# Retention and a bilinear feed-forward layer: another order of loads, transposing DMAs and row stores on SyncE for groups 3 to 10

## The chip, the cores and the metric

The kernel runs on one core of a Trainium2 chip. The metric is the device time of one execution in microseconds (us). Before the change it was 328.05 us, the median of three runs (327.72 to 330.47). TensorE (PE) multiplies matrices into PSUM, VectorE (DVE), ScalarE (ACT) and GpSimd (POOL) do the elementwise work, and SyncE (SP) issues most of the DMAs, in program order.

## The reference

```python
# q, k, v: (8, 8, 576, 64) float32, batch x heads x positions x head_dim
scores = scale * q @ k.transpose(0, 1, 3, 2)
gamma = 1.0 - 2.0 ** (-5.0 - arange(8))
Dmat = where(rel >= 0, gamma[:, None, None] ** rel, 0.0)   # rel = pos[:, None] - pos[None, :]
x = (scores * Dmat) @ v                # to (4608 tokens, 512)
out = ((x @ w_a) * (x @ w_b)) @ w_out  # w_a, w_b: 512 x 1536, w_out: 1536 x 512; out float32
```

## The kernel before

The 4608 tokens are handled in 18 groups of 256 tokens. A group is half of a batch (128 positions twice), except that groups 15 and 17 gather the last 64 positions of four batches each. Groups 0 to 2 are done at the start in another way (the names with `step`), and the others one at a time. The feed-forward layer runs over blocks of tokens: 512, 256, 256, and then seven times 512. In each block twelve rounds of four products `pa` (L745) and four products `pb` (L760) of 128x128 by 512 (or 256) columns give the hidden rows `hT`, and then twelve products `po` (L779) for each 128 tokens give a row block of the output.

Retention is done in chunks of 64 positions. For each group from 3 on these steps are needed:

- `load_pair(n, which)` issues on SyncE the loads of q, k and v into float32 tiles `qf`, `kf`, `vf` (L148): two DMAs of 256 KB for each of the three, one for each 128 rows (`kp`), four for the groups 15 and 17. Each name has four buffers.
- `ahead(n)` casts them on GpSimd to bf16: the lower 64 partitions of q and k as they are (L480), the upper 64 with neighbouring heads exchanged (`upper`, L477), and v scaled by the decay into `vb` (L485). `qkb` and `vb` have three buffers. For k of group 4 the upper half is kept back and cast later by ScalarE, in `upper_keys`.
- `turn(n)` issues two transposing DMAs on SyncE, `qkT` from `qkb`, for q and for k (L498). From group 9 on it also issues the loads of group n + 2 (and for group 9 those of k and v of group 10). `qkT` has three buffers.
- `stretch(into, outof)` is the work of TensorE: for the group `outof`, products with the running states (`open_outputs`, L624); for the group `into`, the key-value sums `kv` (`keyed`, L534) and the scores `sc` (`matched`, L596), the only step that first needs `qkT` of that group; then the products of `outof` with its masked scores (`close_outputs`, L637). What VectorE and ScalarE have to do for it (adding sums, masking, casting states, scaling into `xT`) is put into the list `later`, and is taken from it one entry at a time between the feed-forward products (`pop`).
- `store` writes 128 rows of the output. Rows of blocks 0 to 2 are held back in eight `osb` buffers, and `store_held(rows)` writes them later. In groups 0 to 2 a row block goes out as two DMAs of 128 KB (L701), later as one of 256 KB (L703).

Where these steps stand between the feed-forward products is written out by hand in the list `todo`: a position, counted in products of 512 columns (144 for a block of 512 tokens), and a function. The main loop (from L947) emits the products and runs each entry at the next permitted place (after a `pb` round, or after every fourth `po`) at or beyond its position. The tables `casts` and `turns` give the positions of `ahead` and `turn`. All entries for SyncE, with the stores, form one queue in the order in which they are emitted, and a DMA that must wait for its operand holds back all behind it.

Of the kernel before, what the change touches and what calls it, by code (L numbers as in the profile page):

```python
# [18 lines left out]
def kernel(  # L19
# [10 lines left out]
    nc = tc.nc  # L30

    B, H, S, D = q.shape
    DM = H * D
# [11 lines left out]
    NP = NTOK // 256  # L45
# [12 lines left out]
    def part_of(n):  # L58
        return PAIRS[n][1]
# [106 lines left out]
    Q, K, V = 0, 1, 2  # L166
# [292 lines left out]

        return 8 if n in LEFT else 4 * part_of(n) + i  # L460

    kept = []

    def upper_keys():
        kept.pop()()

    def ahead(n):


        qf, kf, vf = (paired[n].pop(i) for i in (Q, K, V))  # L470
        qkb = nat.tile([128, 2, 2 * DM], BF16, tag="qkb", name="qkb2")
        vb = nat.tile([128, 2 * DM], BF16, tag="vb", name="vb2")
        def upper(w, t, copy):
            to = qkb[64:128, w].rearrange("p (j r d) -> p j r d", r=2, d=D)
            fro = t[64:128].rearrange("p (j r d) -> p j r d", r=2, d=D)
            for r in (0, 1):
                copy(to[:, :, 1 - r], fro[:, :, r])  # L477

        for w, t in ((0, qf), (1, kf)):
            nc.gpsimd.tensor_copy(qkb[0:64, w], t[0:64])  # L480
            if (n, w) == (4, 1):
                kept.append(lambda: upper(1, kf, nc.scalar.copy))
            else:
                upper(w, t, nc.gpsimd.tensor_copy)
        nc.gpsimd.tensor_tensor(  # L485
            vb.rearrange("p (k h d) -> p k h d", k=2, h=H),
            vf.rearrange("p (k h d) -> p k h d", k=2, h=H),
            vs2[:, 2 if n in LEFT else part_of(n)].unsqueeze(3)
            .to_broadcast([128, 2, H, D]),
            op=ALU.mult)  # L490
        natural[FIRST + n, "pair"] = (qkb, vb)
# [417 lines left out]
    def turn_step(i):  # L909
# [3 lines left out]
    todo = [(100, early_casts, ()), (112, turn_step, (4,)),  # L913
            (112.1, cast_step, (5, Q, "act")), (116, score_step, (4,)), (116, state_step, (4,)),
            (124, turn_step, (5,)), (128, output_step, (4,)),
            (128, score_step, (5,)), (128, state_step, (5,)),
            (140, output_step, (5,))]
# [1 line left out]
    todo += [(136, total_of, (2,))]  # L919
    todo += [(28 + 6 * step, pair_tables, (step,)) for step in range(13)]  # L920
    todo += [(170, stretch, (3, None)), (197, stretch, (4, 3)),
             (248, stretch, (5, 4)), (274, open_alone, (5,)),
             (278, close_outputs, (5,)), (336, stretch, (6, None)),
             (372, stretch, (7, 6)), (408, stretch, (8, 7))]
    for n in range(8, NP, 2):
# [3 lines left out]
                 (starts[n] - 44, open_alone, (n + 1,))]  # L929
    todo += [(starts[NP - 2] - 40, close_outputs, (NP - 1,))]  # L930
    placed = {args[0]: at for at, fn, args in todo if fn is stretch}
    casts = {3: 116, 4: 116.15, 5: 175.3, 6: 200, 7: 250, 8: 330}
    turns = {3: 116, 4: 175.1, 5: 175.4, 6: 200.2, 7: 272, 8: 345}
    loads = {9: 345.1}
    todo += [(116.1, load_pair, (4, (K, V))), (175, upper_keys, ()),
             (175.2, load_pair, (5,)), (175.5, load_pair, (6,)), (200.1, load_pair, (7, (Q, K))),
             (200.3, load_pair, (7, (V,))), (200.4, store_held, (4,)),
             (271, load_pair, (8, (Q,))), (272.1, load_pair, (8, (K, V))),
             (272.2, store_held, (2,)), (345.2, store_held, (2,)),
             (345.3, load_pair, (10, (Q,)))]  # L940
    for n in range(9, NP):
        casts[n], turns[n] = placed[n] - 70, placed[n] - 38
    for fn, places in ((ahead, casts), (turn, turns), (load_pair, loads)):
        todo += [(at, fn, (n,)) for n, at in places.items()]
    todo.sort(key=lambda e: e[0])

# [2 lines left out]
    for tb, n in enumerate(blocks):  # L949
        runs = WCOLS if tb == 0 else [1] * NF  # L950
        for cost, edge in ffn_block(tb, tok, n, runs):
            at += cost
            while todo and edge and at >= todo[0][0]:
                _, fn, args = todo.pop(0)
# [33 lines left out]
```

## Time and profile before

| What | Value |
|---|---|
| Median of three runs (lowest, highest) | 328.05 us (327.72, 330.47) |
| The profiled execution's own time, and its span | 326.78 us, 325.0 us |
| TensorE, share of the span | 98% |
| VectorE, ScalarE, GpSimd, share of the span | 50%, 40%, 36% |
| DMA packets of SyncE's queue | 45.37 MB, 69.4% of 16 engines' span |
| Mean DMA rate | 157 GB/s |
| Granted TensorE clock | 1.0 |

The span runs from the first to the last instruction. One product of 512 columns takes 0.216 us when they follow each other (four in 0.86), so 72 positions of `todo` are some 15.6 us, and more with the retention products between them. The trace gives the start of the first score product of each group and the landing of its second transposing DMA:

| Group | `todo` position of its stretch | qkT of k landed, us | first score product, us |
|---|---|---|---|
| 3 | 170 | 54.99 | 57.02 |
| 4 | 197 | 63.07 | 64.45 |
| 5 | 248 | 74.86 | 76.17 |
| 6 | 336 | 90.70 | 97.87 |
| 7 | 372 | 103.70 | 107.54 |
| 8 | 408 | 114.44 | 116.03 |
| 9 | 460 | 129.66 | 129.71 |
| 10 | 532 | 146.06 | 146.10 |
| 11 | 604 | 160.14 | 163.77 |

A line of a timeline reads: start, time that the merged instructions take together, engine and line, operation, output and inputs, shape, count; in brackets the idle time before it and what ended it. A line of the waits reads: who waited for what, us in total, how often, the longest.

### The profile page before, as it was taken

What the parts mean: (1) busy time and instruction counts of PE and PEld (TensorE: products, weight loads), DVE (VectorE), ACT (ScalarE), POOL (GpSimd) and SP (SyncE); (2) the same over time, 40 slices, a digit from 0 to 9 for tenths busy, and PEclk for the clock granted to TensorE, in tenths of its full rate; (3) what the DMA queues carried; (4) which work ended last, traced back from release to release, by engine and by line L of the source; (5) the groups of instructions that cost most, each with busy time, mean ns of one, the idle gap of its engine ahead of it and who ended that gap; (6) DMA issues with size and microseconds to landing.
All of it is one profiled execution on the core that took longest, in us unless ns stands there. A gap on an engine that the chain in (4) does not pass through costs nothing.

```text
span 325.0 us, 8647 instructions
## 1 busy us (share of the span) xinstructions
PE 318.7 (98%) x3611; PEld 164.5 (51%) x3611; DVE 161.6 (50%) x288; ACT 129.5 (40%) x286; POOL 115.5 (36%) x148
## 2 busy tenths in 40 slices
PE   7899999999999999999999999999999999999996
PEld 3564457778444554444454545454445444444444
DVE  6734454665437754735374626561556245414321
ACT  7745753663435533533253324442333233212321
POOL 4990077374642554575274205440520000000000
PEclk9999999999999999999999999999999999999999
DMA  8999999999999999999899169935840620031013
GB/s 217 255 197 207 261 229 200 199 164 216 172 225 200 218 235 243 208 226 229 177 214 194 48 163 199 212 69 145 204 73 22 112 66 0 2 97 32 0 23 109
DMA packets 145431, 50.90 MB, mean 157 GB/s; under 512 B 126704, under 2 KB 140912, under 8 KB 145392
## 3 DMA queue, kind: packets, MB, share of 16 engines
q1 hardware_dynamic: 140112, 45.37, 69.4%
q0 software_dynamic: 4752, 4.72, 8.9%
q8 instruction: 28, 0.46, 0.6%
q10 hardware_dynamic: 528, 0.26, 0.3%
q14 instruction: 11, 0.09, 0.1%
HBM read 37.75 MB, written 9.44 MB: 145 GB/s over the span
## 4 chain that ended last, share of the span: by engine, by line
PE 78%; SPq 9%; DMA 7%; POOL 2%; DVE 1%; issue 1%; ACT 1%; DVEq 0%; ACTq 0%; POOLq 0%
PE po L779 26%; PE pb L760 23%; PE pa L745 22%; SPq L148 5%; DMA qf<-in_q_dram 3%; DMA kf<-in_k_dram 3%; SPq L159 2%; SPq L498 2%; DMA qkT<-qkb 1%; PE o L637 1%; PE o L624 1%; POOL qkb L480 1%; PE sc L596 1%; PE pa L722 1%; POOL qkb L477 1%
## 5 line engine op out<-in xcount | busy, mean ns | idle before, releaser
L765 DVE TENSOR_TENSOR hT<-ha,pb 128x512 bf16<-128x512 bf16 (+1 forms) x120 | 75.9, 634 | 98.0 <-PE pb L760 89.9
L753 ACT CAST ha<-pa 128x512 bf16<-128x512 f32 (+1 forms) x120 | 64.7, 543 | 120.1 <-PE pa L745 117.2
L760 PE MATMUL pb<-xT,wb_sb 128*128 128x512 bf16 (+1 forms) x480 | 111.5, 358 | 0.2
L745 PE MATMUL pa<-xT,wa_sb 128*128 128x512 bf16 (+1 forms) x468 | 108.8, 357 | 0.0
L779 PE MATMUL po<-wo_sb,hT 128*128 128x512 bf16 (+2 forms) x456 | 97.5, 368 | 0.0
L760 PEld LDWEIGHTS <-wb_sb 128*128 128x128 bf16 x480 | 46.9, 98 | 46.8 <-issue 0.5
L745 PEld LDWEIGHTS <-wa_sb 128*128 128x128 bf16 x468 | 45.0, 98 | 44.4 <-issue 0.2
L779 PEld LDWEIGHTS <-hT 128*128 128x128 bf16 x456 | 42.5, 98 | 46.5
L480 POOL CAST qkb<-qf 64x1024 bf16<-64x1024 f32 x15 | 15.5, 1031 | 68.3 <-DMA qf<-in_q_dram 68.3
L485 POOL TENSOR_TENSOR vb<-vf,vs 128x1024 bf16<-128x1024 f32 x15 | 28.5, 1903 | 14.9 <-PE pa L745 7.0
L790 DVE COPY osb<-po 128x512 f32<-128x512 f32 (+2 forms) x17 | 11.1, 652 | 40.4 <-PE po L779 40.4
L788 ACT COPY osb<-po 128x512 f32<-128x512 f32 (+1 forms) x21 | 12.0, 570 | 44.8 <-PE po L779 44.8
L647 DVE TENSOR_TENSOR xT<-o,qs 128x512 bf16<-128x512 f32 x30 | 19.5, 682 | 4.9 <-PE o L637 4.9
L480 POOL CAST qkb<-kf 64x1024 bf16<-64x1024 f32 x15 | 15.8, 1055 | 16.1 <-DMA kf<-in_k_dram 15.6
L559 DVE TENSOR_TENSOR sums<-kv,sums 128x256 f32<-128x256 f32 x44 | 18.6, 424 | 2.8 <-PE kv L534 0.8
L605 DVE TENSOR_TENSOR sT<-sc,mask 128x512 bf16<-128x512 f32 x30 | 19.4, 680 | 0.0
L477 POOL CAST qkb<-qf 64x512 bf16<-64x512 f32 x30 | 17.6, 616 | 0.7
L477 POOL CAST qkb<-kf 64x512 bf16<-64x512 f32 x28 | 16.5, 616 | 0.8
L563 ACT CAST states<-sums 64x512 bf16<-64x512 f32 x26 | 16.0, 617 | 0.3
L311 POOL CAST qkb<-kf 128x512 bf16<-128x512 f32 x5 | 3.1, 617 | 16.8 <-DMA kf<-in_k_dram 16.8
L664 ACT COPY fence<-o 128x2 f32<-128x2 f32 x15 | 2.4, 161 | 15.5 <-PE o L624 15.5
L806 PE MATMUL w<-ones 128*128 128x512 bf16 x19 | 6.9, 483 | 1.5 <-DVE idxp_f L204 1.5
(84 smaller groups left out, 158.4 us busy)
## 6 DMA issues: line engine op xcount, KB each, us to landing
qf<-in_q_dram SPq DMA_DIRECT2D x32, 256.0 KB, 4.7
vf<-in_v_dram SPq DMA_DIRECT2D x32, 256.0 KB, 5.2
kf<-in_k_dram SPq DMA_DIRECT2D x31, 256.0 KB, 5.0
out_dram<-osb SPq DMA_DIRECT2D x25, 256.0 KB, 3.3
out_dram<-osb SPq DMA_DIRECT2D x21, 128.0 KB, 2.4
wo_sb<-in_moe_w_out_dram POOLq DMA_DIRECT2D x3, 512.0 KB, 16.9
qf<-in_q_dram SPq DMA_DIRECT2D x8, 128.0 KB, 3.2
kf<-in_k_dram SPq DMA_DIRECT2D x8, 128.0 KB, 3.4
```

The lines of the kernel that those rows point to most:

```text
L148: nc.sync.dma_start(t[r0:r0 + m, kp * DM:(kp + 1) * DM] .rearrange("p (h d) -> p h d", h=H), src[b, :, s0:s0 + m, :].rearrange("h s d -> s ...
L477: copy(to[:, :, 1 - r], fro[:, :, r])
L480: nc.gpsimd.tensor_copy(qkb[0:64, w], t[0:64])
L485: nc.gpsimd.tensor_tensor(vb.rearrange("p (k h d) -> p k h d", k=2, h=H), vf.rearrange("p (k h d) -> p k h d", k=2, h=H), vs2[:, 2 if n in ...
L559: nc.vector.tensor_tensor(sums[:, i], own, prev, op=ALU.add)
L605: nc.vector.tensor_tensor(sT[:, on].rearrange("p c k s -> p (c k) s"), sc[:, on].rearrange("p c k s -> p (c k) s"), mask3.unsqueeze(1).to_ ...
L647: nc.vector.tensor_tensor(x_of(t0, 128).rearrange("p c (a s) -> p c a s", a=2), o[:, :, :, kp].rearrange("p a c s -> p c a s"), qs[:, :, s ...
L745: nc.tensor.matmul(pa[:, 0:n], wa_sb[:, c, fs], xT[:, c], start=(c == 0), stop=(c == NC - 1))
L753: nc.scalar.copy(ha[:, 0:n], pa[:, 0:n])
L760: nc.tensor.matmul(pb[:, 0:n], wb_sb[:, c, fs], xT[:, c], start=(c == 0), stop=(c == NC - 1))
L765: nc.vector.tensor_tensor(hT[:, F, 0:n], has[F][:, 0:n], pb[:, 0:n], op=ALU.mult)
L779: nc.tensor.matmul(po[:, 0:width], hT[:, F, u * 128:(u + 1) * 128], wo_sb[:, F, cols], start=(F == 0), stop=(F == NF - 1))
```

## The change

Only positions and one cast are changed; every load, transposing DMA, store and product is still made once.

- The order on SyncE. Before: T4 (the two transposing DMAs of group 4), loads of 5, T5, loads of 6, q and k of 7, T6, v of 7, the four held row blocks of block 0, q of 8, T7, k and v of 8, the two row blocks of block 1, T8, loads of 9, the two of block 2, q of 10, three row blocks of block 3, T9, k and v of 10, loads of 11, the last row block of block 3, T10. After: T4, loads of 5, q of 6, T5, k and v of 6, q and k of 7, T6, a row block, v of 7, a row block, q of 8, a row block, k of 8, a row block, v of 8, T7, the two row blocks of block 1, T8, loads of 9, q of 10, the two of block 2, T9, k and v of 10, loads of 11, four row blocks of block 3, T10.
- `casts` and `turns` have the positions that go with it; those of groups 10 and later are the same.
- The cast of k of groups 4 and 5 is made in two halves, each for the 512 columns of one load, with the lower and the two upper casts of a half before those of the next. All are on GpSimd; `upper_keys` on ScalarE is gone.
- The stretch of groups 5 and 4 is placed at 252 instead of 248, that is, after one more round of `pa` and `pb` in a block of 256 tokens.

```diff
@@ -459,29 +459,21 @@
 
         return 8 if n in LEFT else 4 * part_of(n) + i
 
-    kept = []
-
-    def upper_keys():
-        kept.pop()()
-
     def ahead(n):
 
 
         qf, kf, vf = (paired[n].pop(i) for i in (Q, K, V))
         qkb = nat.tile([128, 2, 2 * DM], BF16, tag="qkb", name="qkb2")
         vb = nat.tile([128, 2 * DM], BF16, tag="vb", name="vb2")
-        def upper(w, t, copy):
-            to = qkb[64:128, w].rearrange("p (j r d) -> p j r d", r=2, d=D)
-            fro = t[64:128].rearrange("p (j r d) -> p j r d", r=2, d=D)
-            for r in (0, 1):
-                copy(to[:, :, 1 - r], fro[:, :, r])
-
         for w, t in ((0, qf), (1, kf)):
-            nc.gpsimd.tensor_copy(qkb[0:64, w], t[0:64])
-            if (n, w) == (4, 1):
-                kept.append(lambda: upper(1, kf, nc.scalar.copy))
-            else:
-                upper(w, t, nc.gpsimd.tensor_copy)
+            runs = 2 if (n, w) in ((4, 1), (5, 1)) else 1
+            for i in range(runs):
+                e = slice(i * 2 * DM // runs, (i + 1) * 2 * DM // runs)
+                nc.gpsimd.tensor_copy(qkb[0:64, w, e], t[0:64, e])
+                to, fro = (x.rearrange("p (j r d) -> p j r d", r=2, d=D)
+                           for x in (qkb[64:128, w, e], t[64:128, e]))
+                for r in (0, 1):
+                    nc.gpsimd.tensor_copy(to[:, :, 1 - r], fro[:, :, r])
         nc.gpsimd.tensor_tensor(
             vb.rearrange("p (k h d) -> p k h d", k=2, h=H),
             vf.rearrange("p (k h d) -> p k h d", k=2, h=H),
@@ -919,7 +911,7 @@
     todo += [(136, total_of, (2,))]
     todo += [(28 + 6 * step, pair_tables, (step,)) for step in range(13)]
     todo += [(170, stretch, (3, None)), (197, stretch, (4, 3)),
-             (248, stretch, (5, 4)), (274, open_alone, (5,)),
+             (252, stretch, (5, 4)), (274, open_alone, (5,)),
              (278, close_outputs, (5,)), (336, stretch, (6, None)),
              (372, stretch, (7, 6)), (408, stretch, (8, 7))]
     for n in range(8, NP, 2):
@@ -929,18 +921,20 @@
                  (starts[n] - 44, open_alone, (n + 1,))]
     todo += [(starts[NP - 2] - 40, close_outputs, (NP - 1,))]
     placed = {args[0]: at for at, fn, args in todo if fn is stretch}
-    casts = {3: 116, 4: 116.15, 5: 175.3, 6: 200, 7: 250, 8: 330}
-    turns = {3: 116, 4: 175.1, 5: 175.4, 6: 200.2, 7: 272, 8: 345}
-    loads = {9: 345.1}
-    todo += [(116.1, load_pair, (4, (K, V))), (175, upper_keys, ()),
-             (175.2, load_pair, (5,)), (175.5, load_pair, (6,)), (200.1, load_pair, (7, (Q, K))),
-             (200.3, load_pair, (7, (V,))), (200.4, store_held, (4,)),
-             (271, load_pair, (8, (Q,))), (272.1, load_pair, (8, (K, V))),
-             (272.2, store_held, (2,)), (345.2, store_held, (2,)),
-             (345.3, load_pair, (10, (Q,)))]
-    for n in range(9, NP):
+    casts = {3: 116, 4: 116.15, 5: 141, 6: 200, 7: 253, 8: 283, 9: 376}
+    turns = {3: 116, 4: 116.2, 5: 141.2, 6: 200.2, 7: 253.1, 8: 283.1, 9: 380}
+    todo += [(116.1, load_pair, (4, (K, V))), (116.3, load_pair, (5,)),
+             (141.1, load_pair, (6, (Q,))), (141.3, load_pair, (6, (K, V))),
+             (200.1, load_pair, (7, (Q, K))), (200.3, store_held, (1,)),
+             (200.4, load_pair, (7, (V,))), (200.5, store_held, (1,)),
+             (200.6, load_pair, (8, (Q,))), (200.7, store_held, (1,)),
+             (200.8, load_pair, (8, (K,))), (200.9, store_held, (1,)),
+             (201, load_pair, (8, (V,))), (253.2, store_held, (2,)),
+             (283.2, load_pair, (9,)), (345, load_pair, (10, (Q,))),
+             (345.1, store_held, (2,))]
+    for n in range(10, NP):
         casts[n], turns[n] = placed[n] - 70, placed[n] - 38
-    for fn, places in ((ahead, casts), (turn, turns), (load_pair, loads)):
+    for fn, places in ((ahead, casts), (turn, turns)):
         todo += [(at, fn, (n,)) for n, at in places.items()]
     todo.sort(key=lambda e: e[0])
```

## The prediction

> **What bounds the kernel.** I read the busy shares first, then what TensorE waited for, then the stretches around those waits, and only then SyncE's queue, which the change reorders.
>
> ```profile
> PE 318.7 (98%) x3611; PEld 164.5 (51%) x3611; DVE 161.6 (50%) x288; ACT 129.5 (40%) x286; POOL 115.5 (36%) x148
> ```
>
> TensorE is busy for 98% of the span, so what can be won is what it still waits for:
>
> ```profile
> PE w L806 <- DVE idxp_f L204: 1.5, 1, 1.5
> PE sc L343 <- ACT qkT L330: 0.5, 2, 0.2
> PE sc L596 <- DMA qkT<-qkb: 0.4, 2, 0.3
> ```
>
> The first two lie in the opening 16 us, which the change does not touch. The third does: two times a group's score products (L596) wait for a transposing DMA. Those two are groups 9 and 10. The timeline of TensorE shows group 9, and then group 11, which waits for nothing:
>
> ```profile
> 127.90 1.03 PE L760 MATMUL pb<-xT,wb_sb 128*128 128x512 bf16 x4
> ...
> 129.71 0.45 PE L596 MATMUL sc<-qkT 64*64 64x64 bf16 x32 [0.16 <-DMA qkT<-qkb]
> ...
> 130.35 0.82 PE L745 MATMUL pa<-xT,wa_sb 128*128 128x512 bf16 x3
> ```
>
> ```profile
> 162.30 1.03 PE L760 MATMUL pb<-xT,wb_sb 128*128 128x512 bf16 x4
> ...
> 163.77 0.50 PE L596 MATMUL sc<-qkT 64*64 64x64 bf16 x32
> ...
> 164.49 0.82 PE L745 MATMUL pa<-xT,wa_sb 128*128 128x512 bf16 x3
> ```
>
> From the last four projection products to the first ones after the stretch it is 2.45 us for group 9 (127.90 to 130.35) and 2.19 us for group 11. Group 10 takes 2.58 (144.17 to 146.75), group 8 2.29; undisturbed stretches take 2.19 to 2.30 (groups 7, 11, 12, 13, 14). The waits are therefore worth 0.25 + 0.38 + 0.1 = 0.7 us against 2.20, and 0.4 against 2.30, which is the figure of the wait row. The chain that ended last runs from 94 to 146 us through SyncE's issues, loads and casts, but TensorE is busy beside it: a faster queue wins no more than those 0.4 to 0.7 us.
>
> **The change, part by part.** I follow the second transposing DMA of each group, "Tn", against the score products that need it. Before, they landed / were needed at: T4 63.07 / 64.45, T5 74.86 / 76.17, T6 90.70 / 97.87, T7 103.70 / 107.54, T8 114.44 / 116.03, T9 129.66 / about 129.5, T10 146.06 / about 145.8. These are thin margins, so each reordering is worked out by what it puts ahead of Tn. Three prices, from landings in a busy stretch: a load of 256 KB 1.15 us (group 6: 76.47, 77.67, 78.88, 80.05), a half store of 128 KB 0.31 landing to landing (93.69, 94.00, 94.31) but 0.63 to issue, a transposing DMA 0.8 to 0.9.
>
> *T4 and the casts of k by halves.* SyncE's order is unchanged to the end of group 5's loads. What changes is who casts:
>
> ```profile
> 57.91 1.04 POOL L480 CAST qkb<-kf 64x1024 bf16<-64x1024 f32 x1 [2.38 <-DMA kf<-in_k_dram]
> 61.51 1.91 POOL L485 TENSOR_TENSOR vb<-vf,vs 128x1024 bf16<-128x1024 f32 x1 [2.56 <-PE pa L745]
> ...
> 69.35 1.03 POOL L480 CAST qkb<-kf 64x1024 bf16<-64x1024 f32 x1 [1.21 <-DMA kf<-in_k_dram]
> 70.44 1.18 POOL L477 CAST qkb<-kf 64x512 bf16<-64x512 f32 x2
> ```
>
> A 64x512 cast takes 0.616 and a 64x1024 one 1.035, so a column costs 0.82 ns and an instruction 0.2 us; 64x256, which the trace lacks, comes to 0.4 (GpSimd's 128x256 cast in L393 takes 0.40). A half is 0.62 + 2 x 0.40 = 1.4 us. Group 4's halves of k landed at 56.62 and 57.79: the first half runs 56.7 to 58.1, the second to 59.5. Before, ScalarE's two copies ended at 59.57. T4 is where it was; if the small casts cost 0.62 like the larger, it is 0.9 later and still within 1.4 of cover. GpSimd has 1.8 us more to do, inside its 2.56 us gap before the values. ScalarE loses two copies of 0.61 just before an evacuation that came late: at 60.90 to 61.59 four products took 0.69 where 0.44 is usual. That is worth 0 to 0.25; I take 0.1.
>
> One rule of the Trainium skill speaks against casts on GpSimd: Advanced Engine Details and Errata, Mode Summary, says that the second VectorE port is shared with GpSimd, and that two-port VectorE work and GpSimd block each other. The 64x512 casts here took 616 ns on average for q and for k, beside a VectorE half busy. By the rule T4 could slip by some of its cover; by the rows it does not.
>
> *T5 and the later stretch.* SyncE stands still for T5 before:
>
> ```profile
> 64.31 3.35 SPq L148 DMA_DIRECT2D vf<-in_v_dram  x2
> 68.16 4.74 SPq L498 DMA_TRANSPOSE qkT<-qkb  x2
> 72.94 1.25 SPq L148 DMA_DIRECT2D qf<-in_q_dram  x2
> ```
>
> Of those 4.74 us two issues of 1.3 to 1.8 are work, the rest waits for GpSimd's cast that ends at 71.63. Two loads of group 6 now fill that hole. With the halves the cast runs 68.15 to 69.6 and, k's second half having landed at 69.23, to 71.0. T5 then issues at about 70 and 71.8 and lands at 75.1 to 75.5; if nothing of the hole were used, at 74.86 + 2 x 1.15 = 77.2. The stretch that needs it moves by one pair of 256-column groups, 0.88 us (pb at 74.23 and 75.11): needed at 77.05. What was behind the stretch has one slot less: the four adds, two scalings and two masked copies were done at 83.55 before, which becomes about 84.2; the products that need them start at 85.03. ScalarE's state casts end near 83.0 instead of 83.14, and are read at 83.69. No new stall, but margins of 0.7 and 0.8.
>
> SyncE is at the same place as before at 73.1, two loads ahead: 2.3 us won.
>
> *T6.* The same set of DMAs lies ahead of it: at most 90.70, about 88; needed at 97.87.
>
> *T7.* Four loads of group 8 now lie ahead of it: at most 103.70 + 4 x 1.15 = 108.3, which would be 0.8 late. Against that stand the 2.3 us from T5 and the way the eight half stores are spread:
>
> ```profile
> 89.91 5.99 SPq L701 DMA_DIRECT2D out_dram<-osb  x8
> 95.96 1.30 SPq L148 DMA_DIRECT2D qf<-in_q_dram  x2
> ```
>
> Eight stores took 5.99 us to issue and some 2.6 to move: the DMA share falls to 0.91 in 88 to 96 us, from 1.16 to 1.27 around it. Put between loads, the four store pairs cost little but their 2.6 us. T7 lands at 108.3 - 2.3 - 2.4 = 103.6; 4 us of cover.
>
> The page DMA: Bandwidth & Descriptors, under "Issuing engines are not separate DMA queues", says that the time to issue is usually small beside the transfer. By that rule the interleaving wins nothing and T7 comes at 106.0, still in time; the eight stores above are the opposite case.
>
> *T8, T9, T10.* T8 follows T7 after four half stores (2.5) and two transposings, with its operands long loaded: about 109.5, or 114 with T7 at its bound; needed at 116.03. T9 has the same DMAs ahead of it as before less three stores of block 3 (at least 1.1 by their issue of 0.38), and the wins above: 122 to 128.5; needed at 129.5. T10 keeps its distance to T9 (16.4 us) plus three stores (2): 140, and 145.8 or so from the later bound. So the waits of groups 8 and 9 go for certain, that of group 10 almost so. From T11 on SyncE stands behind block 4's stores, as before (the last issued at 154.47 after ScalarE), and nothing changes.
>
> **Sum.** -0.25 -0.38 (less 0.1 for the 2.30 reading) -0.1 (group 8) -0.1 (ScalarE) = -0.7 us, with bounds of -1.1 and 0 from the rows alone. On the profiled execution: 326.78 - 0.7 = 326.1. Its own time is 1.3 below the median of the three runs, so for the median 328.05 - 0.7, rounded to 327.3. This measurement tells about 1%, 3.3 us, from no change; the forecast is inside that.
>
> **Rivals.**
> 1. *Transposing DMAs late behind loads (slower).* T5 at its bound of 77.2 is 0.1 late. Now and then a load lands 2.3 us after its neighbour instead of 1.15 (66.91 to 69.23, 99.44 to 102.03); one such in front of T5 makes it 1.3 late, and T7 at its bound adds 0.8. That is +2.1 - 0.7 = +1.4: 329.4. It is slower than before from 0.7 us of lateness, and over 1% from 4 us, for which several groups would have to fail. For it: thin margins, three runs spread by 2.7 us. Against: SyncE's idle hole at T5 is seen in the rows, and the moved stretch.
> 2. *No difference.* Groups 9 and 10 still come late by other means (T10's bound), or what TensorE stops waiting for is lost to the slot that the stretch gave up: 328.0.
> 3. *A larger gain.* If the runs that lie 1 to 3.7 us above the profiled execution are slower because T3 to T10 come late in them, wider margins take most of that away: 328.05 - 2 = 326.0.
>
> **Chances.** Forecast 0.58 (326.8 to 327.8), no difference 0.15, larger gain 0.09 (a third of it beyond 1%), slower 0.18 (a third of it beyond 1%). Range: down to the larger gain, 325.8, up past the slower rival, 329.6. Faster by over 1% 0.03, slower by over 1% 0.06, the rest within.
>
> **What would show it.** Right: no wait of L596 for a transposing DMA; the stretches of groups 8 to 10 at 2.2 to 2.3 us; T9 before 129; the transposing pair near 70 us no longer 4.74 us. Wrong: a wait of L596 for T5 at 77 or T7 near 107; L624 waiting for states near 84; or the median moving by more than TensorE's waits do, which would mean that the executions differ in something that the profile of before does not show.

## The result, and the profile after

| | before | after |
|---|---|---|
| Median of 22 executions each, us (lowest, highest) | 329.22 (327.72, 332.0) | 327.48 (326.04, 332.47) |
| Ratio, with its 95% interval | | 0.9952 (0.9929 to 0.9975) |
| The profiled execution, us (span) | 326.78 (325.0) | 327.25 (325.5) |

The kernel is about 0.5% faster, within the 1% that the prediction could not tell from no change, and the time is 0.2 us from the one forecast. Two things do not fit so well. The gain is 1.6 us by the ratio and not 0.7, and the two profiled executions stand the other way round: that of after is 0.5 us longer. The executions of one kernel differ by several microseconds, and the profiled one of before was faster than all 22 in the table.

The busy shares of after, and what TensorE waited for:

```profile
PE 319.0 (98%) x3611; PEld 165.2 (51%) x3611; DVE 162.5 (50%) x288; ACT 128.3 (39%) x284; POOL 117.2 (36%) x156
```

```profile
PE w L798 <- DVE idxp_f L204: 1.5, 1, 1.5
PE sc L588 <- DMA qkT<-qkb: 1.1, 1, 1.1
PE sc L343 <- ACT qkT L330: 0.5, 2, 0.3
```

(The lines have moved by eight: L596 is now L588, L498 is L490.) The score products wait once instead of twice, but longer, 1.1 us against 0.4. TensorE's timeline around the stretches of groups 9 and 10 says which one it is:

```profile
127.80 1.03 PE L752 MATMUL pb<-xT,wb_sb 128*128 128x512 bf16 x4
...
129.27 0.50 PE L588 MATMUL sc<-qkT 64*64 64x64 bf16 x32
129.99 1.04 PE L737 MATMUL pa<-xT,wa_sb 128*128 128x512 bf16 x4
```

```profile
143.82 1.03 PE L771 MATMUL po<-wo_sb,hT 128*128 128x512 bf16 x4
...
146.60 0.45 PE L588 MATMUL sc<-qkT 64*64 64x64 bf16 x32 [1.11 <-DMA qkT<-qkb]
...
147.24 1.04 PE L771 MATMUL po<-wo_sb,hT 128*128 128x512 bf16 x4
```

Group 9 has an undisturbed stretch of 2.19 us (127.80 to 129.99); group 10 takes 3.42 (143.82 to 147.24), 1.2 too long. SyncE's timeline shows why, from group 5 on:

```profile
65.26 3.25 SPq L148 DMA_DIRECT2D vf<-in_v_dram  x2
68.55 1.78 SPq L148 DMA_DIRECT2D qf<-in_q_dram  x2
70.50 4.64 SPq L490 DMA_TRANSPOSE qkT<-qkb  x2
75.19 1.26 SPq L148 DMA_DIRECT2D kf<-in_k_dram  x2
...
122.69 3.66 SPq L490 DMA_TRANSPOSE qkT<-qkb  x2
126.41 1.20 SPq L148 DMA_DIRECT2D kf<-in_k_dram  x2
127.65 2.12 SPq L148 DMA_DIRECT2D vf<-in_v_dram  x2
129.82 2.29 SPq L148 DMA_DIRECT2D qf<-in_q_dram  x2
132.16 3.52 SPq L148 DMA_DIRECT2D kf<-in_k_dram  x2
135.72 2.31 SPq L148 DMA_DIRECT2D vf<-in_v_dram  x2
138.12 2.67 SPq L695 DMA_DIRECT2D out_dram<-osb  x4
140.90 3.36 SPq L490 DMA_TRANSPOSE qkT<-qkb  x2
```

Two readings matter. The pair of transposing DMAs of group 5 takes 4.64 us to issue, as against 4.74 before: SyncE stands there as long as it did, only 2.3 us later (for another reason than before, see T5 below). And between the pairs of groups 9 and 10 stand ten loads and four stores, 14.5 us of issues (126.41 to 140.90).

### The profile page after: what moved, and what is told of

The parts are those of the page before. It is cut to its first block, busy times and chain, and to the rows that moved or that the text cites. A ratio compares the mean times of both kernels' runs of the same rounds, so it can differ in the third digit from the quotient of the medians.

```text
span 325.5 us, 8652 instructions
## 1 busy us (share of the span) xinstructions
PE 319.0 (98%) x3611; PEld 165.2 (51%) x3611; DVE 162.5 (50%) x288; ACT 128.3 (39%) x284; POOL 117.2 (36%) x156
## 4 chain that ended last, share of the span: by engine, by line
PE 84%; DMA 5%; SPq 4%; POOL 2%; ACT 2%; issue 1%; DVE 1%; POOLq 0%; ACTq 0%; DVEq 0%
PE po L771 26%; PE pb L752 25%; PE pa L737 24%; DMA vf<-in_v_dram 4%; SPq L148 2%; SPq L490 2%; PE w L798 1%; DMA qkT<-qkb 1%; PE o L616 1%; PE o L629 1%; PE sc L588 1%; POOL vb L477 1%; PE tp L328 1%; PE kv L526 1%; PE pa L714 1%
## 5 line engine op out<-in xcount | busy, mean ns | idle before, releaser
L757 DVE TENSOR_TENSOR hT<-ha,pb 128x512 bf16<-128x512 bf16 (+1 forms) x120 | 75.9, 634 | 98.0 <-PE pb L752 90.2
L752 PE MATMUL pb<-xT,wb_sb 128*128 128x512 bf16 (+1 forms) x480 | 111.5, 358 | 0.1
L472 POOL CAST qkb<-kf 64x1024 bf16<-64x1024 f32 (+1 forms) x17 | 15.9, 933 | 15.2 <-DMA kf<-in_k_dram 14.5
L476 POOL CAST qkb<-kf 64x512 bf16<-64x512 f32 (+1 forms) x34 | 18.3, 566 | 1.0
L351 DVE TENSOR_TENSOR sT<-sc,mask_s 128x1024 bf16<-128x1024 f32 x6 | 7.3, 1223 | 2.5 <-PE sc L343 2.5
```

The costliest lines, as they stand in the source:

```text
L472: nc.gpsimd.tensor_copy(qkb[0:64, w, e], t[0:64, e])
L476: nc.gpsimd.tensor_copy(to[:, :, 1 - r], fro[:, :, r])
L752: nc.tensor.matmul(pb[:, 0:n], wb_sb[:, c, fs], xT[:, c], start=(c == 0), stop=(c == NC - 1))
L757: nc.vector.tensor_tensor(hT[:, F, 0:n], has[F][:, 0:n], pb[:, 0:n], op=ALU.mult)
```

## The experiments

**The account of one execution.** All 14 profiles of this study follow one sum. From the start of the first feed-forward product to the end of the last it takes TensorE 304.65 us plus what the retention stretches were late (304.9 with the casts of before, where four products near 61 us came 0.25 late). The rest, the opening and the end, is 21.1 to 22.4 us and differs from execution to execution; the rows below are of several chips. "Late" is the difference to 304.65 or 304.9, that is, what is left over; the waits that the traces name at these groups are 0.1 to 0.4 us shorter (in t10_sooner no wait is named). The last column says where TensorE lost most of it.

| Kernel | profiled execution, us | first product starts, us | first to last product, us | late, us | of it at group |
|---|---|---|---|---|---|
| before | 326.78 | 16.46 | 305.72 | 0.8 | 9, 10 |
| b_again (before) | 327.40 | 16.52 | 306.28 | 1.4 | 9 |
| b_third (before) | 328.06 | 16.50 | 306.94 | 2.0 | 9 |
| b_fourth (before) | 328.94 | 17.12 | 307.24 | 2.3 | 9 |
| after | 327.25 | 16.58 | 306.10 | 1.45 | 10 |
| a_again (after) | 326.52 | 16.88 | 305.06 | 0.4 | 10 |
| early_only | 328.56 | 17.43 | 306.57 | 1.9 | 9 |
| late_only | 327.47 | 16.83 | 306.07 | 1.2 | 10 |
| t10_sooner | 326.34 | 16.83 | 304.91 | 0.3 | 4, 7 |
| t10_again | 326.15 | 16.88 | 304.70 | 0.05 | none |
| late_t10 | 327.69 | 17.49 | 305.62 | 0.7 | 7 |
| t10_no_shift | 327.03 | 17.33 | 305.14 | 0.5 | 5 |
| t10_whole_casts | 327.39 | 17.17 | 305.66 | 1.0 | 4 |
| t10_64_more | 327.10 | 17.86 | 304.66 | 0 | none |

**Was the profile of before typical?** b_again, b_third and b_fourth are the kernel before, unchanged.

> The kernel before once more, for a second profile: its executions spread from 327.7 to 332.0 and the profiled one, 326.78, lay below them all. Theory A (lateness of the transposing DMAs differs from execution to execution): a profile at 328 to 330 shows 1 to 3 us of score products waiting for transposing DMAs, at groups among 4, 5, 8, 9, 10. Theory B (the spread lies elsewhere, in the opening or the last stores): waits of the score products stay at 0.4 us, and the difference stands before 16 us or after 150 us.

> The kernel before, for a third profile: the two so far, 326.78 and 327.4, are faster than its median of 328.4 to 329.2. Theory A: at 328 or more, waits of score products for transposing DMAs of 2 us or more in all, most of it at group 9 or 10. Rival: the opening is later by as much.

> The kernel before, for a fourth profile, with the same expectations as the third.

Measured: 327.40, 328.06 and 328.94 us. The waits of TensorE that name a transposing DMA, in b_third and then in b_fourth:

```profile
PE sc L596 <- DMA qkT<-qkb: 1.6, 1, 1.6
```

```profile
PE sc L596 <- DMA qkT<-qkb: 2.2, 1, 2.2
```

It is always group 9, by 1.1, 1.6 and 2.2 us, where the first profile had 0.16. Theory A holds in kind: the executions differ in how late T9 is. "2 us or more" was met once and missed once, and 0.6 us of b_fourth's length is the opening (first product at 17.12 against 16.5), so the rival has a share. b_again, which came out below 328, decides nothing by its own terms but shows the same place.

**The changed kernel again** (a_again).

> The changed kernel, for a second profile. Theory A: group 9 does not wait, group 10 does, by 0.3 to 2 us, and no other group by more than 0.3; its time less the wait of group 10 is 326.0 to 326.4. Rival (group 10's wait was chance): no wait of group 10.

Measured: 326.52 us, group 10 waiting 0.26 and no other group waiting. That group 10 waits is a property of the order (late_only has it too, below), and the size differs as group 9's did before. It is not that T10 comes later: it lands at 145.8 us here, 146.8 in late_only and 146.6 in after by its wait, and at 146.1 to 147.2 in the four profiles of before. There TensorE had been held up at group 9 and came to group 10 later; without that wait it is there near 145.5, ahead of T10. So a part of what is won at group 9 is lost again at group 10. Less its wait a_again takes 326.3, as theory A said.

**One half of the order at a time.** early_only has groups 4 to 6, the halves and the later stretch of after, late_only groups 7 to 10:

```diff
 # early_only, against after: groups 7 to 10 as before
-    casts = {..., 7: 253, 8: 283, 9: 376}
-    turns = {..., 7: 253.1, 8: 283.1, 9: 380}
+    casts = {..., 7: 253, 8: 330}
+    turns = {..., 7: 272, 8: 345}
+    loads = {9: 345.1}     # and the loads and stores of before from 200.1 on
 # late_only, against before: groups 7 to 10 as after
-    casts = {..., 7: 250, 8: 330}
-    turns = {..., 7: 272, 8: 345}
+    casts = {..., 7: 253, 8: 283, 9: 376}
+    turns = {..., 7: 253.1, 8: 283.1, 9: 380}    # and the loads and stores of after from 200.1 on
```

> The order of groups 4 to 6, the casts by halves and the later stretch alone; groups 7 to 10 as before. Theory A1 (the gain of 1.6 us comes from groups 7 to 10, whose transposing DMAs stood behind stores and later loads): no more than 0.4 us below the kernel before, ratio 0.999 to 1.001. Theory A2 (it comes from group 5's hole on SyncE, which lets everything behind it come earlier): 1 us or more below, ratio 0.995 to 0.997.

> The order of groups 7 to 10 alone; groups 4 to 6, the casts and the stretch as before. Theory A1: most of the gain, ratio 0.995 to 0.997, and no wait of group 9's score products. Theory A2: ratio 0.998 to 1.001.

Measured: early_only 327.14 us, ratio 0.9944 (0.9909 to 0.9979); late_only 327.70, ratio 0.9948 (0.9912 to 0.9984). Neither can be told from both together, 0.9952, so A1 does not stand (early_only gains too much), and A2 hardly (late_only gains too, if its interval just reaches 0.998). The profiles say what each leaves: early_only still has group 9 wait, 1.5 us in an execution of 328.56, the third longest of its twelve; late_only has group 9 in time and group 10 wait 1.0. That gives the gain of late_only in kind and not in size: it is 1.2 us late, and the four profiles of before 1.6 on average. Why the early half makes most executions faster (seven of twelve lie at 327.2 or below) while its profiled one is late at group 9 as before, these runs do not settle; 0.25 us of it is the ScalarE copies that are gone (below).

**Group 10 sooner** (t10_sooner, and t10_again, the same kernel in a second series). The transposing DMAs of group 10 go ahead of the loads of k and v of group 11 and of one of block 3's four stores (the expectation says two):

```diff
+    casts[10], turns[10] = 409, 421
 # in turn(n)
         if n == 9:
             load_pair(10, (K, V))
+            load_pair(11, (Q,))
+        elif n == 10:
+            load_pair(11, (K, V))
+            load_pair(12)
-        if n >= 9:
+        elif n > 10:
             load_pair(n + 2)
```

> The changed kernel with group 10's transposing DMAs ahead of the k and v loads of group 11 and of two of block 3's stores. Its profile had group 10's score products wait 1.1 us. Theory A (that wait is real in most executions): 0.7 to 1.3 us below the changed kernel, ratio to before 0.991 to 0.993, the wait of group 10 gone. Rival (the wait moves to group 11, whose loads come later, or the profile showed an unlucky execution): as the changed kernel, ratio 0.994 to 0.997.

> The kernel of t10_sooner unchanged, as the base of this series: its executions lay within 0.9 us of each other, where those of before spread over 5, so parts can be told apart on it. Both theories: 326.4, again with a spread of 1 us or less; if the spread is 3 us or more, the narrow one was chance.

Measured: 326.35 us (325.83 to 326.73), ratio 0.9905 (0.987 to 0.9939), and again 326.05 (325.64 to 326.74), ratio 0.9936 (0.9907 to 0.9964). It is faster than before; by the medians it is also 1.1 and 1.4 us below the changed kernel, as theory A said, but that one was timed in another series, and the intervals of the ratios overlap. The executions of t10_sooner lie within 0.9 and 1.1 us, where those of before at the same granted clock (0.999 or 1.0) spread over 2.1 and 3.4 in the two series. SyncE's and TensorE's timelines:

```profile
129.81 2.33 SPq L148 DMA_DIRECT2D qf<-in_q_dram  x2
132.23 3.46 SPq L699 DMA_DIRECT2D out_dram<-osb  x3
135.79 3.21 SPq L490 DMA_TRANSPOSE qkT<-qkb  x2
139.06 1.25 SPq L148 DMA_DIRECT2D kf<-in_k_dram  x2
```

```profile
144.11 1.03 PE L775 MATMUL po<-wo_sb,hT 128*128 128x512 bf16 x4
145.60 0.50 PE L592 MATMUL sc<-qkT 64*64 64x64 bf16 x32
146.32 1.04 PE L775 MATMUL po<-wo_sb,hT 128*128 128x512 bf16 x4
```

The pair is issued at 135.8 instead of 140.9 and lands 4.7 us before it is needed; group 10's stretch is 2.21 us. Group 11, whose loads came later, does not wait. With T9 and T10 in time the spread is gone, so it comes for the most part from how late these two are.

The granted clock belongs to this. In these two series 10 of 25 and 12 of 35 executions of before have a granted clock of 0.995 or less, and they take 329.7 us or more; all others take 329.5 or less. Of after it is 2 of 22, of early_only 1 of 12, of late_only 3 of 12, and none of the 56 of this and the next three kernels, which have group 10 sooner. By an estimate a clock lower by 0.5% costs 1.6 of 326 us. Without these executions the medians are 328.19 and 327.91 for before and 327.34 for after: 0.6 to 0.9 us, near the 0.7 forecast. The rest of the 1.6 us would then lie in how many executions have the lower clock; for those of before in the first table the clock is not on record. What lowers it stays open: every profile here was taken at 0.999 or more.

**The parts, on this steadier base.** Differences are of medians of twelve executions each in one series, against t10_again; the intervals come from resampling those executions.

late_t10 has groups 4 to 6, casts and stretch of before, and t10_sooner's order from group 7 on:

> The base with the order of groups 4 to 6, the whole casts with ScalarE's part, and the stretch at 248 taken back to those of before: only groups 7 to 10 differ from the kernel before, with group 10 sooner. Theory A3 (time is lost at groups 9 and 10 alone; the early part of the change is worth nothing once these are in time): within 0.3 us of the base. Theory A2 (the early part has a gain of its own): 0.7 us or more above the base, and executions spread by more than 2 us.

Measured: 326.58, +0.53 us (-0.1 to +1.1), between the two theories. Its profile shows a wait that neither named, group 7's:

```profile
109.31 0.45 PE L600 MATMUL sc<-qkT 64*64 64x64 bf16 x32 [0.54 <-DMA qkT<-qkb]
```

t10_no_shift puts the stretch back:

```diff
-             (252, stretch, (5, 4)), (274, open_alone, (5,)),
+             (248, stretch, (5, 4)), (274, open_alone, (5,)),
```

> The base with the stretch of groups 5 and 4 at 248 again. Group 5's second transposing DMA landed at 77.0 in the profiles of the changed order, and the score products would need it at 76.2 to 76.4. Theory: 0.6 to 0.9 us above the base, with a wait of group 5's score products of that size. Rival (the wait is taken up by the narrow 256-column rounds behind it, whose own stalls shrink): within 0.3 us.

Measured: 326.89, +0.84 us (+0.04 to +1.9), executions up to 328.72. Group 5's score products wait, and the stretch is 0.43 too long in the profiled one:

```profile
77.22 0.45 PE L592 MATMUL sc<-qkT 64*64 64x64 bf16 x32 [0.28 <-DMA qkT<-qkb]
```

So the later stretch is needed with this order, as T5 lands at 77.2 there; what it is worth is hardly clear of nothing, and the wait in this execution is half of what was expected.

t10_whole_casts casts k of groups 4 and 5 in one piece on GpSimd:

```diff
-            runs = 2 if (n, w) in ((4, 1), (5, 1)) else 1
+            runs = 1
```

> The base with the casts of k of groups 4 and 5 in one piece each, all on GpSimd. Group 4's second transposing DMA started when the second half's cast ended (60.15), so it comes about 0.8 later, within what is left before the score products at 64.4: theory: a wait of group 4 of 0 to 0.6 us, time 0 to 0.6 us above the base. Group 5's DMA started 2 us after its cast's end, so nothing there. Rival (the halves matter for group 5): a wait of group 5 of 0.5 us or more.

Measured: 326.53, +0.48 us (-0.2 to +0.9), so not told from nothing. The wait in its profile is another than expected, group 4's key-value sums for its values:

```profile
65.32 0.44 PE L530 MATMUL kv<-vb,qkb 64*64 64x64 bf16 x32 [0.60 <-POOL vb L477]
```

The values' cast itself waited 2.04 us for its load in that execution, so the whole cast is not shown to be its cause. What the halves are worth stays open.

**What holds up SyncE's loads** (t10_64_more). In the DMA records of the profiles 28 packets of 16 KB come on the instruction queue (the page's "q8 instruction: 28, 0.46, 0.6%"), each taking 0.9 to 1.8 us. Now and then a load on SyncE takes over 1.9 us to issue instead of 0.6 to 1.2. The edit makes TensorE reload at other times:

```diff
-    warm(8, 512)
+    warm(4, 512)
+    warm(64, 32)
```

> The base (group 10 sooner) with 64 small products of 32 columns in place of four large ones in the opening, before TensorE has any data: 60 more products and 60 more weight loads, so that TensorE's instructions, which are loaded in packets of 16 KB, are reloaded at other times. In all profiles so far such packets came at about 59, 66, 71, 79, 87, 100, 109, 118, 125, 133 and 148 us, and the SyncE issues of more than 1.9 us at 57, 66, 70, 79, 84, 86, 100, 109, 117, 132, 147. Theory C (a packet holds up one of the DMA engines, and with it SyncE's queue): the packets come at other times, and the long issues with them. Rival (the long issues belong to certain DMAs of the queue): the packets move, and the long issues stay with the same DMAs. Time within 0.5 us of the base, not timed for its own sake.

Starts of the packets and of the loads over 1.9 us, between 50 and 150 us:

```
t10_again    packets 59.4 66.3 72.6 79.3 86.8 99.4 109.5 117.0 125.1 132.3 146.9
             loads   78.6 117.1 146.7 (stores: 132.1)
t10_64_more  packets 54.8 62.4 68.2 79.0 83.0 94.1 106.7 111.5 119.6 132.6 143.6 148.8
             loads   55.0 67.7 79.2 111.5 119.6 132.9 142.8 148.6
```

With the 120 instructions more there are 29 packets instead of 28, so the packets are TensorE's. The long loads moved with them. Of the four DMAs that were long in t10_again two, the store at 132.1 and the load at 146.7, take 0.7 and 1.1 us here, and the load just ahead of each is long instead; those at 111.5 and 142.8 are long for the first time (0.6 and 1.1 in t10_again). The other two, at 78.6 and 117.1, are long in both (79.2 and 119.6), and in both a packet starts within them. Over all 14 profiles, between 40 and 240 us, 72 of 73 loads and stores over 1.9 us have a packet's start inside them or up to 1.5 us ahead, but only 132 of the 1756 shorter ones. Of the transposing DMAs over 1.9 us 73 of 107 have one, and 34 do not. So theory C holds for loads and stores, as far as the place of the packets goes, and the rival for a part of the transposing DMAs. The time, 327.10, is 1.0 us above the base and not within 0.5 as expected; all of it is the opening (first product at 17.86 instead of 16.88), and from there on it is the base.

## Why the prediction was right, and where it was not

- **The bound and the size.** "A faster queue wins no more than those 0.4 to 0.7 us" was right for the execution it was read from and wrong for the median. The term that was mis-sized is the wait of group 9: 0.25 us in the profile of before, 1.1 to 2.2 in the next three. The third rival, with a chance of 0.09, had named this ("T3 to T10 come late in them"). It is what the profiles show at T9, less what group 10 still loses; for the executions at the lower clock no profile shows it. That the time came out right is luck: the gain was larger, and the median of before, 328.05 of three runs then, was 329.22 of 22. The 326.1 for the profiled execution was missed, with 327.25 and 326.52: group 10 still waits, and in the second the opening is 0.4 longer.
- **T9.** "The wait of group 9 goes for certain" held: no wait of group 9 in the two profiles of after, in late_only, or in the six profiles with group 10 sooner. It is not far from waiting: where its landing is recorded in these, T9 lands 0.4 to 1.9 us before it is needed.
- **T10.** "140, and 145.8 or so from the later bound" took the wrong end, and its sum does not come out: 128.5 for T9, the distance of 16.4 and 2 for the stores make 146.9, over 1 us late. So the prediction's own terms had the wait of group 10 as a case, and "almost so" for its end was too sure. The distance itself was right: in a_again T9 lands at 127.5 and T10 at 145.8. The pair lands at 145.8 and 146.6 and is needed near 145.5. The early end was out of reach because the wins ahead of it came only in part (T5 and T7 below).
- **T5.** "SyncE is at the same place as before at 73.1, two loads ahead" was wrong: it is there at 75.2. The first DMA of the pair, before and after:

```profile
68.16 1.83 SPq L498 DMA_TRANSPOSE qkT<-qkb  x1
```

```profile
70.50 3.29 SPq L490 DMA_TRANSPOSE qkT<-qkb  x1
```

Before, the second one then waited for GpSimd's cast, which ended at 71.62, and started at 71.65. After, the cast ends at 71.81, not at the 71.0 forecast, since that of q began at 66.66 instead of 65.89. The second DMA does not wait for it: it starts only at 73.89, because the first takes 3.29 us to issue, with a reload packet at 71.6 inside it. In t10_64_more, the one profile of this order in which no packet falls into the pair, it takes 3.43 us; in the others 3.84 to 4.64. The win of 2.3 us is not to be seen at T6 either: it lands at 90.2 to 91.4 with the new order, and at 90.7 to 91.4 in the four profiles of before. T5 landed at 77.08, near the bound of 77.2, and the moved stretch, needing it at 77.0, kept that to 0.15 us; t10_no_shift shows what it would have been otherwise.

- **T7.** "4 us of cover" was 0.9 to 1.5 where the landing is recorded, at 106.2 to 107.3 instead of 103.6, and in late_t10 T7 was 0.54 late. The stores did win something: from T6 to T7 it is 15.9 to 16.2 us, and it was 12.6 to 13.1 before, while four loads at 1.15 would have added 4.6. That is 1 to 1.8 us of the 2.4, unless the loads cost less there. What did not come is the 2.3 us from T5. The rule of the page DMA: Bandwidth & Descriptors ("Issuing engines are not separate DMA queues"), that issue time is usually small, gave 106.0 and so is nearer than my 103.6, but by two misses that offset each other: it counts on the 2.3 us and leaves out what the stores won.
- **The casts.** GpSimd's timeline for group 4's k:

```profile
57.28 0.61 POOL L472 CAST qkb<-kf 64x512 bf16<-64x512 f32 x1 [1.52 <-DMA kf<-in_k_dram]
57.95 0.75 POOL L476 CAST qkb<-kf 64x256 bf16<-64x256 f32 x2
58.74 0.61 POOL L472 CAST qkb<-kf 64x512 bf16<-64x512 f32 x1
59.39 0.75 POOL L476 CAST qkb<-kf 64x256 bf16<-64x256 f32 x2
```

A half takes 1.4 us, as worked out from the row of another shape, and T4 stays where it was. The casts take 0.61 us as before. VectorE works beside them in every run, so no run here shows what the shared port costs that Advanced Engine Details and Errata names in its Mode Summary. ScalarE's relief was worth its upper bound: the four products that took 0.69 us at 60.90 take 0.44 now, 0.25 against the 0.1 taken.
- **The later stretch.** No wait near 84 us, as said.

## What to carry to other kernels

Where an engine is busy for 98% and its few waits hang on a queue with margins of 1 us, one profile shows which places are at risk, not what they cost: four profiles of one kernel wait at the same place by 0.16 to 2.2 us. A reordering is then worth what it does to those margins, and here a narrow spread of the times was as good a sign of it as the median. Taking away one wait brings TensorE sooner to the next place with a thin margin, so look there too. Before counting on a hole in a queue, ask what else can fill it: the pair at group 5 took about as long when its wait for the cast was gone, and the cure that worked, group 10's DMAs ahead of loads that were not urgent, needed no hole.

## What was not expected of the hardware

TensorE's own instructions take DMA time: 16 KB packets, one each 4 to 17 us while the stretches run, each taking 0.9 to 1.8 us. The loads and stores of SyncE that take 1.9 to 2.9 us to issue instead of about 1 nearly all meet one (72 of 73), though not each that meets one is long. The Trainium skill, DMA: Bandwidth & Descriptors, under "Queues, rings and completion order", says that one copy is split over up to 16 engines and that an engine turns between its queues at packet boundaries; that would make a whole load wait for the one engine, and fits these rows, but no run here looked at the single engine.
